# Pooled attention and a top-1 mixture of experts: one half of the values leaves undivided and is scaled after the gather

## The chip, the cores and the metric

The kernel runs on one core of a Trainium2 chip. The metric is the device time of one execution in microseconds (us), as the median of several runs. Five engines work side by side, each through its own instructions in order: TensorE (PE; PEld is its weight load), VectorE (DVE), ScalarE (ACT), GpSimd (POOL) and SyncE (SP, which here issues transfers). PE writes its sums to PSUM; DVE and ACT read them there, and POOL works on tiles in SBUF and issues the indirect transfers. L614 stands for line 614 of the kernel.

## The reference

Attention over keys and values that are averaged in groups of 8, then a mixture of experts in which each token goes to the one expert with the highest logit:

```python
# q, k, v: 8 batches x 8 heads x 576 x 64
k_p = k.reshape(B, H, 72, 8, D).mean(axis=3)
v_p = v.reshape(B, H, 72, 8, D).mean(axis=3)
scores = (q @ k_p.T) / sqrt(64); scores -= scores.max(-1)
attn = exp(scores); attn /= attn.sum(-1) + 1e-9
x = (attn @ v_p) -> 4608 tokens x 512 (the 8 heads side by side)

logits = x @ w_gate + modality_bias[modality_id]      # 8 experts
e_idx = argmax(logits); gate_w = softmax(logits)[e_idx]
for e in range(8):
    mask = e_idx == e
    h = max(x[mask] @ w1[e], 0)                       # 512 -> 1024
    out[mask] = gate_w[mask] * (h @ w2[e])            # 1024 -> 512
```

## The kernel before, in words

**Attention, about 0 to 192 us.** The 4608 tokens are 36 tiles of 128. Two batches make nine tiles and five steps (`steps`): four steps of two tiles, and in the middle one step of a single tile that holds the last 64 tokens of both batches. There are 20 steps. The order of the work is written out by hand in a loop `for n in range(N + 1)`, which in step `n` computes the scores of step `n` and the values of the tiles of step `n - 1` (`old[0]` and, if there are two, `old[1]`). Each engine runs its instructions in the order in which this loop issues them.

For one tile the stages are: `s_pe` (PE: scores, L520 or L526), `s_dve` (DVE: maximum L533, subtraction L536), `s_act` (ACT: exponentials L548 and L549), `t_pe` and `t_act` (PE transposes the exponentials, L555; ACT copies them from PSUM, L560), `t4_pe` and `t4_act` (the same for the fourth part of the keys, L567 and L574), and then `a_pe` and `x_dve`. `a_pe` multiplies with the values on PE: per bank of PSUM two multiplications L590 and one L594. There are two banks, `av0` for heads 0 to 3 and `av1` for heads 4 to 7, each a tile of its own with one buffer. For each head a bank holds 64 sums of values, 8 sums of logits (the values were multiplied by the gate's weights beforehand, in `v_gate`) and the sum of the exponentials.

`x_dve` divides on DVE, for each bank: L610 takes the sums of the exponentials times 8, L612 their reciprocals, L614 the 256 values times the reciprocals into a row `xb`, L616 the 32 logits times the reciprocals. Between them `gap` lets the next operations of the routing through (`drip`, DVE's list of routing work). SP stores the finished rows of `xb`, 528 columns wide, to a table `xs` in DRAM (L625); columns 512 to 527 hold the gate value and otherwise nothing that is used.

`v_gate`, once per batch, multiplies the pooled values with the gate's weights on PE into a spare part of a bank of scores, and writes them beside the values: two ACT instructions, and L387 on DVE for the fourth part. The next scores of that bank (L520 or L526) wait until these have read it. POOL folds the raw keys and values into their sums (L296 to L298).

**Experts, about 192 to 625 us.** The tokens are sorted by expert into slots of 256. The first two slots take tokens of the first 18 tiles (the groups 0 and 1, `EARLY_GROUPS` = 2) and are gathered while attention still runs. For every later slot POOL gathers the rows from `xs` by index, two indirect transfers of 128 rows (L142), at piece `f == 0` of the slot before (for slot 2 at `f == 3`). A slot has eight pieces `f`; each is the first layer (`hidden`, L162) and the second (`second`, L1143) on PE. At `f == 5` (`f == 6` for slot 2) PE transposes the next slot's rows (`x_transposes`, L153), and ACT and DVE split them into a high and a low part (L155, L156). ACT and DVE also split the weights of the next slot (L135, and L138 on DVE, 128 x 1024). POOL scatters the results (L1129).

Of the kernel before, what the change touches and what calls it, by code (L numbers as in the profile page):

```python
# [9 lines left out]
F32 = mybir.dt.float32  # L10
# [5 lines left out]
ALU = mybir.AluOpType  # L16
# [6 lines left out]
P = 128  # L23
SLOT = 256
EARLY_GROUPS = 2
# [5 lines left out]
def kernel(  # L31
# [37 lines left out]

    xs = dram.tile([NTOK, XW], F32, name="xs")  # L70

# [15 lines left out]
    xg = [cp.tile([P, XW], F32, name=f"xg{i}") for i in range(4)]  # L87
# [52 lines left out]
    def gather(s, idx, col, xgs, rows=NTOK):  # L140
        for tt in range(2):
            nc.gpsimd.indirect_dma_start(  # L142
                out=xgs[(2 * s + tt) % len(xgs)], out_offset=None, in_=xs[0:rows, :],
                in_offset=IndirectOffsetOnAxis(idx[:, col + tt:col + tt + 1].bitcast(U32), 0),
                bounds_check=rows - 1, oob_is_err=False)

    def x_transposes(s, xgs, tts=(0, 1)):
        a, b = xh[s % len(xh)], xl[s % len(xl)]
# [34 lines left out]
    with ExitStack() as actx:  # L183
        ap = actx.enter_context(tc.tile_pool(name="ap", bufs=1))

        late_p = actx.enter_context(tc.tile_pool(name="late_p", bufs=1))
        ps_av = actx.enter_context(tc.tile_pool(name="ps_av", bufs=1, space=PSUM))
# [166 lines left out]
        m4b = m_4.rearrange("p (j o) -> p j o", o=1)  # L354
# [19 lines left out]
        def v_gate(b):  # L374
            vt, vt4 = vts[b]
            dw, d4 = vw[b % NB], v4[b % NB]
            if b:
                pg = spare[1][:, 1, 4 * SPL:4 * SPL + 12 * E].rearrange("p (u x) -> p u x", u=3)
            else:
                pg = ps_tr.tile([P, 3, 4 * E], F32, tag="tr", name=f"pg_{b}")  # L380
            for u in range(2):
                nc.tensor.matmul(pg[:, u, :], vt[:, u, :], wgb[:, u].rearrange("p g x -> p (g x)"), start=True, stop=True)
            nc.tensor.matmul(pg[:, 2, :], vt4, wg[0:64, 1::2, :], start=True, stop=True)
            pgv = pg[:, 0:2, :].rearrange("p u (g a e) -> p (u g) a e", g=2, a=2)
            nc.scalar.activation(dw[:, :, 0, HD:HD + E], pgv[:, :, 0, :], AF.Copy, scale=m_a)
            nc.scalar.activation(dw[:, :, 1, HD:HD + E], pgv[:, :, 1, :], AF.Copy, scale=m_b)
            nc.vector.tensor_tensor(d4[:, :, HD:HD + E], pg[:, 2, :].rearrange("p (j e) -> p j e", j=NPAIR),  # L387
                                    m4b.to_broadcast([P, NPAIR, E]), op=ALU.mult)


        bias_all = ap.tile([P, NT, E], F32, name="bias_all")
# [89 lines left out]
        qts, pqs, scs, pes, pps, pts, avs, lgs = {}, {}, {}, {}, {}, {}, {}, {}  # L481
# [94 lines left out]
        def a_pe(t):  # L576
            n, z = tile_step[t]
            b, jj, _ = steps[n]
            pt, pt4 = pts.pop(t), pt4z[z]
            av = [ps_av.tile([P, 512], F32, tag=f"av{u}", name=f"av_{t}_{u}") for u in range(2)]  # L580
            avs[t] = av
            if jj is not None:
                halves = [(slice(0, P), b % NB)]
            else:
                halves = [(slice(64 * y, 64 * y + 64), (b - 1 + y) % NB) for y in range(2)]
            for u in range(2):
                for gg in range(2):
                    c = 2 * u + gg
                    for hs, y in halves:
                        nc.tensor.matmul(av[u][hs, 2 * VC * gg:2 * VC * (gg + 1)], pt[:, c, hs],  # L590
                                         vw[y][:, c].rearrange("p a x -> p (a x)"), start=(gg == 0), stop=False)
                dst4 = av[u][:, 0:4 * VC].rearrange("p (g x) -> p g x", g=2)[:, :, VC:2 * VC]
                for hs, y in halves:
                    nc.tensor.matmul(dst4[hs], pt4[:, hs], v4[y][:, 2 * u:2 * u + 2, :], start=False, stop=True)  # L594

        def x_dve(t):
            n, z = tile_step[t]
            g, gi = tile_group[t]
            av = avs.pop(t)
            mixed = steps[n][1] is None  # L600
            b = steps[n][0]
            if gi == 0:
                lgs[g] = late_p.tile([P, GT, H, E], F32, tag="lg", bufs=2, name=f"lg_{g}")
            xw = xbs[n if n < NX0 else NX0 + n % (len(xbs) - NX0)]
            xo = xw[:, z, 0:D]
            for u in range(2):
                avv = av[u][:, 0:4 * VC].rearrange("p (h x) -> p h x", h=4)
                r = ap.tile([P, 4], F32, tag="r", bufs=4, name=f"r_{t}_{u}")
                rb = r.rearrange("p (h o) -> p h o", o=1)
                nc.vector.tensor_scalar(r, avv[:, :, VC - 1], float(POOL), 1e-9 * POOL, op0=ALU.mult, op1=ALU.add)  # L610
                gap(1)
                nc.vector.reciprocal(r, r)  # L612
                gap(1)
                nc.vector.tensor_tensor(xo[:, u * D // 2:(u + 1) * D // 2].rearrange("p (h d) -> p h d", h=4), avv[:, :, 0:HD],  # L614
                                        rb.to_broadcast([P, 4, HD]), op=ALU.mult)
                nc.vector.tensor_tensor(lgs[g][:, gi, 4 * u:4 * u + 4, :], avv[:, :, HD:HD + E],  # L616
                                        rb.to_broadcast([P, 4, E]), op=ALU.mult)
# [277 lines left out]
        for n in range(N + 1):  # L895
            has, nxt, nxt2 = n < N, n + 1 < N, n + 2 < N
# [84 lines left out]
    op = [[ps_op.tile([P, 512], F32, name=f"op{i}_{z}") for z in range(2)] for i in range(2)]  # L981
# [75 lines left out]
    def row(a):  # L1057
# [201 lines left out]

    more(NSTAT - 1)  # L1260

# [29 lines left out]
```

## Time and profile before

| what | value |
|---|---|
| median of three runs | 641.79 us (639.85 to 642.85) |
| the profiled execution | 639.47 us, its span 637.8 us, granted clock 0.99 |
| PE busy | 601.1 us, 94% of the span |
| DVE busy | 433.8 us, 68% |
| ACT busy | 343.8 us, 54% |
| POOL busy | 198.9 us, 31% |
| the chain that ended last | PE 76%, DVE 13%, DMA 7% |

The busy share is an average over two phases with different limits, so a stage is read from a table by stretches of time. A row "PE av L590 <- DVE lg L616" in the table of waits says that PE, at line 590, which writes the tile `av`, was released by DVE's line 616. In the groups, "xb<-av,r 128x256" is an operation that writes `xb` from `av` and `r`, with 128 partitions of 256 elements; then come the count, the busy time in us, the mean in ns, and the idle time before. In the timeline the columns are the start, the length, the engine, the line and the operation, and in brackets the idle time before it and what ended it.

### The profile page before, as it was taken

Reading aid. Unit: us, or ns where it says so; the run is one execution under the profiler, and the core shown is the slowest. Engines: PE = TensorE matmul, PEld = TensorE weight load, DVE = VectorE, ACT = ScalarE, POOL = GpSimd, SP = SyncE. Lnnn points to the kernel's source line nnn. Section 1 sums busy time; section 2 is a strip of 40 time slices with the busy share of each in tenths; the row PEclk is TensorE's granted clock in tenths of the full one; section 3 lists DMA queues with packets and bytes.
Section 4 is the critical chain, followed back from the end, with each engine's and each line's share of the span. In section 5 each row is a group of like instructions: output and inputs, shape, how many; then the busy total and the mean of one; then the engine's idle time right before and its main releaser. Section 6 shows DMA issues by size and latency. Waiting matters only on the chain.

```text
span 637.8 us, 12547 instructions
## 1 busy us (share of the span) xinstructions
PE 601.1 (94%) x4223; PEld 544.8 (85%) x4223; DVE 433.8 (68%) x940; ACT 343.8 (54%) x640; POOL 198.9 (31%) x277
## 2 busy tenths in 40 slices
PE   4799898989899999999999999999999999999992
PEld 3699797888798999999999999999999999999881
DVE  4778989999977578666566566656656566656541
ACT  2667566677441455555555555555556555555530
POOL 6689967563000221320320221231131231131230
PEclk9899999999999999999999999999999999999997
DMA  9999979764201901201210461220225410120120
GB/s 255 290 300 337 350 208 362 223 202 143 67 35 51 315 33 36 68 34 35 68 41 28 148 201 51 67 65 8 63 75 180 145 55 17 52 68 18 51 75 17
DMA packets 63406, 77.18 MB, mean 121 GB/s; under 512 B 15455, under 2 KB 42079, under 8 KB 63328
## 3 DMA queue, kind: packets, MB, share of 16 engines
q1 hardware_dynamic: 57168, 55.98, 28.4%
q0 software_dynamic: 6160, 20.26, 9.7%
q8 instruction: 38, 0.62, 0.4%
q14 instruction: 40, 0.33, 0.2%
HBM read 119.94 MB, written 19.45 MB: 219 GB/s over the span
## 4 chain that ended last, share of the span: by engine, by line
PE 76%; DVE 13%; DMA 7%; issue 1%; ACT 1%; SPq 0%; DVEq 0%; ACTq 0%
PE op L1143 30%; PE hp L162 30%; DMA out_dram<-ob,sidx 6%; PE av L590 3%; PE sc L526 3%; PE xt L153 2%; DVE mx L533 2%; DVE sb L536 2%; PE av L594 2%; DVE xb L614 2%; PE pq L501 1%; PE ph L162 1%; PE pp L555 1%; DVE arow L717 1%; DMA k<-in_k_dram 1%
## 5 line engine op out<-in xcount | busy, mean ns | idle before, releaser
L135 ACT CAST hl<-raw 128x1024 fp32r<-128x1024 f32 x138 | 144.8, 1049 | 138.6 <-PE op L1143 136.6
L162 PE MATMUL hp<-xh,hl 128*128 128x256 f32 x1152 | 186.2, 284 | 0.6 <-issue 0.6
L162 PEld LDWEIGHTS hp<-xh,hl 128*128 128x128 f32 x1152 | 166.0, 189 | 11.5 <-issue 1.0
L138 DVE TENSOR_TENSOR hl<-raw,hl 128x1024 fp32r<-128x1024 f32 x144 | 174.8, 1215 | 0.0
L1143 PE MATMUL op<-hl,hh 128*128 128x512 f32 x554 | 173.5, 394 | 0.0
L1129 POOL DMA_INDIRECT out_dram<-ob,sidx x37 | 51.0, 1379 | 369.3 <-DVE ob L1125 260.2
L166 DVE SCALAR_TENSOR_TENSOR hlo<-hp,hh 128x256 fp32r<-128x256 f32 x139 | 58.8, 423 | 136.6 <-ACT hh L164 136.6
L1143 PE MATMUL op<-hl,hlo 128*128 128x512 f32 x277 | 108.4, 391 | 0.0
L1143 PEld LDWEIGHTS op<-hl,hh 128*128 128x128 f32 x554 | 94.8, 189 | 12.1
L162 PE MATMUL hp<-xl,hl 128*128 128x256 f32 x576 | 92.0, 282 | 0.0
L164 ACT ACTIVATE hh<-hp 128x256 fp32r<-128x256 f32 x139 | 53.4, 384 | 49.6 <-PE hp L162 49.6
L162 PEld LDWEIGHTS hp<-xl,hl 128*128 128x128 f32 x576 | 79.0, 190 | 0.0
L1143 PEld LDWEIGHTS op<-hl,hlo 128*128 128x128 f32 x277 | 52.0, 188 | 11.8
L590 PE MATMUL av<-vw,pt 128*128 128x146 f32 (+1 forms) x320 | 50.9, 299 | 4.9 <-DVE lg L616 3.7
L142 POOL DMA_INDIRECT xg<-xs,gidx x40 | 44.2, 1105 | 17.1 <-issue 8.9
L590 PEld LDWEIGHTS av<-vw,pt 128*128 128x128 f32 (+1 forms) x320 | 40.3, 183 | 7.9 <-DVE lg L616 4.9
L526 PE MATMUL sc<-kt,qt 128*128 128x144 f32 x256 | 38.3, 294 | 1.5 <-DVE rs L706 1.1
L526 PEld LDWEIGHTS sc<-kt,qt 128*128 128x128 f32 x256 | 34.1, 195 | 2.4 <-DVE rs L706 1.3
L156 DVE TENSOR_TENSOR xl<-xt,xh 128x512 fp32r<-128x512 f32 x38 | 24.5, 684 | 15.5 <-ACT xh L155 15.5
L560 ACT COPY pt<-pp 128x512 f32<-128x512 f32 x36 | 21.1, 586 | 25.4 <-PE pp L555 25.0
L533 DVE TENSOR_REDUCE mx<-sc 128x8 f32<-128x576 f32 (+1 forms) x40 | 27.7, 692 | 10.0 <-PE sc L526 7.6
L614 DVE TENSOR_TENSOR xb<-av,r 128x256 f32<-128x256 f32 x72 | 30.4, 422 | 1.6
(226 smaller groups left out, 710.5 us busy)
## 6 DMA issues: line engine op xcount, KB each, us to landing
raw<-in_moe_w_dram SPq DMA_DIRECT2D x304, 256.0 KB
xs<-xb SPq DMA_DIRECT2D x16, 528.0 KB
k<-in_k_dram SPq DMA_DIRECT2D x7, 1024.0 KB
v<-in_v_dram SPq DMA_DIRECT2D x7, 1024.0 KB
q<-in_q_dram SPq DMA_DIRECT2D x6, 1024.0 KB
q<-in_q_dram SPq DMA_DIRECT2D x4, 512.0 KB
v<-in_v_dram SPq DMA_DIRECT2D x16, 128.0 KB
xs<-xb SPq DMA_DIRECT2D x8, 132.0 KB
```

The lines of the kernel that those rows point to most:

```text
L135: nc.scalar.copy(hl[f][:, 0, :], raw[f])
L138: eng.tensor_sub(hl[f][:, 1, :], raw[f], hl[f][:, 0, :].bitcast(F32))
L142: nc.gpsimd.indirect_dma_start(out=xgs[(2 * s + tt) % len(xgs)], out_offset=None, in_=xs[0:rows, :], in_offset=IndirectOffsetOnAxis(idx[:, ...
L162: nc.tensor.matmul(ph, hl[f][:, w, d * P:(d + 1) * P], x[:, d, :], start=(n == 0 and d == 0), stop=(n == 2 and d == ND - 1))
L164: nc.scalar.activation(hh, ph, AF.Relu)
L166: nc.vector.scalar_tensor_tensor(hlo, ph, 0.0, hh.bitcast(F32), op0=ALU.max, op1=ALU.subtract)
L526: nc.tensor.matmul(dst, qt[:, i, :], kt[b % NB][:, :, h * SPL:(h + 1) * SPL], start=True, stop=True)
L533: nc.vector.reduce_max(mx, scv, axis=AX.X)
L590: nc.tensor.matmul(av[u][hs, 2 * VC * gg:2 * VC * (gg + 1)], pt[:, c, hs], vw[y][:, c].rearrange("p a x -> p (a x)"), start=(gg == 0), sto ...
L614: nc.vector.tensor_tensor(xo[:, u * D // 2:(u + 1) * D // 2].rearrange("p (h d) -> p h d", h=4), avv[:, :, 0:HD], rb.to_broadcast([P, 4, H ...
L1129: nc.gpsimd.indirect_dma_start(out=out[:, :], out_offset=IndirectOffsetOnAxis(idx.bitcast(U32), 0), in_=ob, in_offset=None, bounds_check=N ...
L1143: nc.tensor.matmul(o[tt], l[:, ts_], hl[f][:, w, D:2 * D], start=(f == 0 and n == 0), stop=(f == NF - 1 and n == 2))
```

## The change

In `x_dve` the two banks become one tile `av` of two banks with one buffer. One scaling, one reciprocal and one logits operation serve all eight heads. The values of heads 4 to 7 are divided by DVE as before. For tiles 0 to 17 so are those of heads 0 to 3; from tile 18 on, that is from the eleventh step, ACT copies these 256 columns into the row undivided, and the eight reciprocals are written to columns 520 to 527 of the row. After the gather, POOL multiplies the 256 columns in place by the row's first four reciprocals (`scale_half`, twice per slot from slot 2 on), at `f == 3` (`f == 5` for slot 2). Rows of early tiles hold the value 1 in those columns. In `v_gate`, DVE's L387 becomes an ACT copy to SBUF and a multiplication on POOL.

```diff
+    RX = D + 8
+    def scale_half(s, xgs):
+        for tt in range(2):
+            x = xgs[(2 * s + tt) % len(xgs)]
+            xv = x[:, 0:D // 2].rearrange("p (h d) -> p h d", h=H // 2)
+            nc.gpsimd.tensor_tensor(xv, xv, x[:, RX:RX + H // 2]...to_broadcast([P, H // 2, HD]), op=ALU.mult)
...
# v_gate
-            nc.vector.tensor_tensor(d4[:, :, HD:HD + E], pg[:, 2, :]..., m4b..., op=ALU.mult)
+            vg4 = ap.tile([P, NPAIR, E], F32, tag="vg4", bufs=1, name=f"vg4_{b}")
+            nc.scalar.copy(vg4, pg[:, 2, :]...)
+            nc.gpsimd.tensor_tensor(d4[:, :, HD:HD + E], vg4, m4b..., op=ALU.mult)
...
-            nc.gpsimd.memset(t[:, :, D:XW], 0.0)
+            nc.gpsimd.memset(t[:, :, D:XW], 1.0)
...
# a_pe
-            av = [ps_av.tile([P, 512], F32, tag=f"av{u}", name=f"av_{t}_{u}") for u in range(2)]
+            av = ps_av.tile([P, 2, 512], F32, tag="av", name=f"av_{t}")
...
# x_dve
-            for u in range(2):
-                avv = av[u][:, 0:4 * VC].rearrange("p (h x) -> p h x", h=4)
-                r = ap.tile([P, 4], F32, tag="r", bufs=4, name=f"r_{t}_{u}")
-                nc.vector.tensor_scalar(r, avv[:, :, VC - 1], float(POOL), 1e-9 * POOL, op0=ALU.mult, op1=ALU.add)
-                gap(1)
-                nc.vector.reciprocal(r, r)
-                gap(1)
-                nc.vector.tensor_tensor(xo[:, u * D // 2:(u + 1) * D // 2]..., avv[:, :, 0:HD], rb..., op=ALU.mult)
-                nc.vector.tensor_tensor(lgs[g][:, gi, 4 * u:4 * u + 4, :], avv[:, :, HD:HD + E], rb..., op=ALU.mult)
+            avv = av[:, :, 0:4 * VC].rearrange("p u (h x) -> p u h x", h=4)
+            s8 = ap.tile([P, 2, 4], F32, tag="r", bufs=4, name=f"r_{t}")
+            late = g >= EARLY_GROUPS
+            r = xw[:, z, RX:RX + H].rearrange("p (u h) -> p u h", u=2) if late else s8
+            nc.vector.tensor_scalar(s8, avv[:, :, :, VC - 1], float(POOL), 1e-9 * POOL, op0=ALU.mult, op1=ALU.add)
+            gap(1)
+            nc.vector.reciprocal(r, s8)
+            gap(1)
+            nc.vector.tensor_tensor(lgs[g][:, gi]..., avv[:, :, :, HD:HD + E], rb..., op=ALU.mult)
+            nc.vector.tensor_tensor(xo[:, D // 2:D]..., avv[:, 1, :, 0:HD], rb[:, 1]..., op=ALU.mult)
+            if late:
+                nc.scalar.copy(xo[:, 0:D // 2]..., avv[:, 0, :, 0:HD])
+            else:
+                nc.vector.tensor_tensor(xo[:, 0:D // 2]..., avv[:, 0, :, 0:HD], rb[:, 0]..., op=ALU.mult)
+            gap(2)
...
# run (a slot of the experts)
+                if f == (5 if s == 1 else 3) and nxt and not early:
+                    scale_half(s + 1, xg)
```

In the changed kernel the lines move: L610, L612, L616 and L614 become L622, L624, L626 and L628 (heads 4 to 7), L631 is ACT's copy of heads 0 to 3, L633 is DVE's division of them for early tiles, and L152 is POOL's scaling.

DVE's order at tile 25, the first of the fifteenth step, before. A row gives line, operation, what it writes and reads (with buffer numbers) and the shape; L782 to L784 are routing operations that `gap` let through:

```order
L610 TENSOR_SCALAR r_0_2194<-av_0_2167 128x4
L782 TENSOR_TENSOR sc_104<-oh,e0oh 128x144
L612 RECIPROCAL r_0_2194<-r_0_2194 128x4
L783 TENSOR_REDUCE s_1630<-sc_104 128x18
L614 TENSOR_TENSOR xb_177<-av_0_2167,r_0_2194 128x256
L616 TENSOR_TENSOR lg_1695<-av_0_2167,r_0_2194 128x32
L610 TENSOR_SCALAR r_1_2201<-av_1_2168 128x4
L784 SCALAR_TENSOR_TENSOR b_1632<-rh,s_1630 128x18
L612 RECIPROCAL r_1_2201<-r_1_2201 128x4
L784 SCALAR_TENSOR_TENSOR b_1632<-rh,s_1630 128x18
L614 TENSOR_TENSOR xb_177<-av_1_2168,r_1_2201 128x256
L616 TENSOR_TENSOR lg_1695<-av_1_2168,r_1_2201 128x32
```

And in the changed kernel, the same tile:

```order
L622 TENSOR_SCALAR r_2082<-av_2056 128x8
L800 TENSOR_TENSOR sc_104<-oh,e0oh 128x144
L624 RECIPROCAL xb_177<-r_2082 128x8
L801 TENSOR_REDUCE s_1550<-sc_104 128x18
L626 TENSOR_TENSOR lg_1614<-av_2056,xb_177 128x64
L628 TENSOR_TENSOR xb_177<-av_2056,xb_177 128x256
L802 SCALAR_TENSOR_TENSOR b_1552<-rh,s_1550 128x18 x4
```

Eight instructions of the tile have become four, one bank's division has left DVE, and the routing operations stand behind the tile rather than in it.

ACT's order behind the second tile of the same step, before; L338 and L339 copy keys, and L560 begins the next step:

```order
L338 COPY kt_134<-pk_1_2249 64x192
L339 COPY kt_134<-pk_1_2249 64x192
L560 COPY pt_2273<-pp_2268 128x512
L548 ACTIVATE pe_2275<-sb_0_2227 128x2x2x128
L549 ACTIVATE pe_2275<-sb_0_2227 128x2x32
L574 COPY pt_0_135<-sc_0_2213 64x128
L574 COPY pt_1_136<-sc_0_2213 64x128
```

And in the changed kernel, where L346 and L347 are the copies of keys, L569 is `t_act`, L557 and L558 are `s_act`, and L583 is `t4_act`:

```order
L631 COPY xb_177<-av_2115 128x256
L346 COPY kt_134<-pk_1_2128 64x192
L347 COPY kt_134<-pk_1_2128 64x192
L569 COPY pt_2152<-pp_2147 128x512
L557 ACTIVATE pe_2154<-sb_0_2111 128x2x2x128
L558 ACTIVATE pe_2154<-sb_0_2111 128x2x32
L583 COPY pt_0_135<-sc_0_2097 64x128
L583 COPY pt_1_136<-sc_0_2097 64x128
```

The copy of the tile's undivided half stands ahead of the next step's work. In the program it waits for L628 of the same tile, which writes the other half of the same row and is the last of DVE's instructions that read `av`; and the next `a_pe` waits for both.

POOL's order in the expert phase, before; `xg` are the gathered rows, and `ob` the results to be scattered:

```order
L1129 DMA out_dram<-ob_1_3402,sidx_95 4608x512
L142 DMA xg_82<-xs,gidx 128x528
L142 DMA xg_83<-xs,gidx 128x528
L1129 DMA out_dram<-ob_0_3638,sidx 4608x512
L1129 DMA out_dram<-ob_1_3643,sidx 4608x512
```

And in the changed kernel:

```order
L1147 DMA out_dram<-ob_1_3240,sidx_95 4608x512
L143 DMA xg_82<-xs,gidx 128x528
L143 DMA xg_83<-xs,gidx 128x528
L152 TENSOR_TENSOR xg_82<-xg_82 128x256
L152 TENSOR_TENSOR xg_83<-xg_83 128x256
L1147 DMA out_dram<-ob_0_3478,sidx 4608x512
L1147 DMA out_dram<-ob_1_3483,sidx 4608x512
```

The two scalings stand between a slot's gather and the scatter of the slot that is then computed. The orders of PE and SP are the same in both kernels.

More of the change, by code (lines that the diff above doesn't have):

```diff
@@ L145, in gather @@
                 bounds_check=rows - 1, oob_is_err=False)
+    def scale_half(s, xgs):
+        for tt in range(2):
+            x = xgs[(2 * s + tt) % len(xgs)]
+            xv = x[:, 0:D // 2].rearrange("p (h d) -> p h d", h=H // 2)
+            nc.gpsimd.tensor_tensor(xv, xv, x[:, RX:RX + H // 2].rearrange("p (h o) -> p h o", o=1).to_broadcast([P, H // 2, HD]),
+                                    op=ALU.mult)
     def x_transposes(s, xgs, tts=(0, 1)):
@@ L386, in v_gate @@
             nc.scalar.activation(dw[:, :, 1, HD:HD + E], pgv[:, :, 1, :], AF.Copy, scale=m_b)
-            nc.vector.tensor_tensor(d4[:, :, HD:HD + E], pg[:, 2, :].rearrange("p (j e) -> p j e", j=NPAIR),
-                                    m4b.to_broadcast([P, NPAIR, E]), op=ALU.mult)
+            vg4 = ap.tile([P, NPAIR, E], F32, tag="vg4", bufs=1, name=f"vg4_{b}")
+            nc.scalar.copy(vg4, pg[:, 2, :].rearrange("p (j e) -> p j e", j=NPAIR))
+            nc.gpsimd.tensor_tensor(d4[:, :, HD:HD + E], vg4, m4b.to_broadcast([P, NPAIR, E]), op=ALU.mult)
         bias_all = ap.tile([P, NT, E], F32, name="bias_all")
@@ L605, in x_dve @@
             xo = xw[:, z, 0:D]
-            for u in range(2):
-                avv = av[u][:, 0:4 * VC].rearrange("p (h x) -> p h x", h=4)
-                r = ap.tile([P, 4], F32, tag="r", bufs=4, name=f"r_{t}_{u}")
-                rb = r.rearrange("p (h o) -> p h o", o=1)
-                nc.vector.tensor_scalar(r, avv[:, :, VC - 1], float(POOL), 1e-9 * POOL, op0=ALU.mult, op1=ALU.add)
-                gap(1)
-                nc.vector.reciprocal(r, r)
-                gap(1)
[L614 to L617, printed above, removed]
+            avv = av[:, :, 0:4 * VC].rearrange("p u (h x) -> p u h x", h=4)
+            s8 = ap.tile([P, 2, 4], F32, tag="r", bufs=4, name=f"r_{t}")
+            late = g >= EARLY_GROUPS
+            r = xw[:, z, RX:RX + H].rearrange("p (u h) -> p u h", u=2) if late else s8
+            rb = r.rearrange("p u (h o) -> p u h o", o=1)
+            nc.vector.tensor_scalar(s8, avv[:, :, :, VC - 1], float(POOL), 1e-9 * POOL, op0=ALU.mult, op1=ALU.add)
+            gap(1)
+            nc.vector.reciprocal(r, s8)
+            gap(1)
+            nc.vector.tensor_tensor(lgs[g][:, gi].rearrange("p (u h) e -> p u h e", u=2), avv[:, :, :, HD:HD + E],
+                                    rb.to_broadcast([P, 2, 4, E]), op=ALU.mult)
+            nc.vector.tensor_tensor(xo[:, D // 2:D].rearrange("p (h d) -> p h d", h=4),
+                                    avv[:, 1, :, 0:HD], rb[:, 1].to_broadcast([P, 4, HD]), op=ALU.mult)
+            if late:
+                nc.scalar.copy(xo[:, 0:D // 2].rearrange("p (h d) -> p h d", h=4), avv[:, 0, :, 0:HD])
+            else:
+                nc.vector.tensor_tensor(xo[:, 0:D // 2].rearrange("p (h d) -> p h d", h=4),
+                                        avv[:, 0, :, 0:HD], rb[:, 0].to_broadcast([P, 4, HD]), op=ALU.mult)
+            gap(2)
             if mixed:
```

4 lines of the change are left out of this document (2 added, 2 removed).

## Prediction

> **What bounds the kernel now.** I began with the table by stages (stretch, length, busy time and instruction count of PE, PEld, DVE, ACT, POOL, granted clock, DMA share, GB/s), then asked each stage which wait of PE ends last, and only then for the durations of the operations that the change touches.
>
> ```profile
> span 637.8 us, 12547 instructions
> 60.00:118.00 58.00, 52.18 (x427) 46.25 (x425) 55.22 (x185) 35.86 (x98) 45.24 (x73) 1.00 0.92 299
> 118.00:160.00 42.00, 39.12 (x348) 35.98 (x347) 40.51 (x137) 32.31 (x82) 17.14 (x26) 1.00 0.60 191
> 160.00:180.00 20.00, 16.82 (x151) 15.48 (x150) 19.37 (x68) 9.06 (x22) 0.00 (x0) 1.00 0.16 43
> 200.00:580.00 380.00, 380.00 (x2520) 345.66 (x2519) 239.23 (x354) 205.81 (x304) 80.11 (x64) 1.00 0.24 79
> ```
>
> There are two regimes. From 60 to 180 us (attention) DVE is busy 115.1 of 120 us and PE leaves 5.8 + 2.9 + 3.2 = 11.9 us idle: this is all that a lighter DVE can win, since in the experts' phase, from 200 to 580 us, PE is full at a clock of 1.00. There every us by which PE is held up is added to the end, and DVE has 37% to spare. The waits of PE in 60 to 180 us (total, times, longest):
>
> ```profile
> PE av L590 <- DVE lg L616: 3.7, 4, 1.3
> PE sc L520 <- DVE vw L387: 3.5, 3, 1.3
> PE sc L526 <- DVE rs L706: 1.1, 1, 1.1
> PE pp L555 <- DVE xl L156: 0.7, 1, 0.7
> PE pp L555 <- DVE h L166: 0.6, 1, 0.6
> ```
>
> Two are touched: the sums av, whose banks DVE must read before PE may write the next tile, and the scores sc, whose bank holds the gate values of `v_gate` until L387 has run. Both name DVE. The last three (2.4 us) belong to routing and to the first expert slot; the change leaves them.
>
> **DVE's part of a tile.** The operations by form (busy, mean ns of one), with the rows nearest to what replaces them:
>
> ```profile
> L614 DVE TENSOR_TENSOR xb<-av,r 128x256 f32<-128x256 f32 x50 | 21.1, 421 | 0.9
> L616 DVE TENSOR_TENSOR lg<-av,r 128x32 f32<-128x32 f32 x50 | 8.9, 179 | 0.0
> L612 DVE RECIPROCAL r<-r 128x4 f32<-128x4 f32 x50 | 8.7, 174 | 0.8
> L610 DVE TENSOR_SCALAR r<-av 128x4 f32<-128x4 f32 x50 | 7.5, 149 | 0.0
> L370 ACT COPY vt<-pv 128x256 f32<-128x256 f32 x5 | 1.9, 373 | 0.1
> L361 POOL TENSOR_TENSOR vw<-vp,m 128x256 f32<-128x256 f32 x5 | 3.0, 607 | 7.0 <-PE pk L332 7.0
> ```
>
> A tile costs DVE 2 x (149 + 174 + 421 + 179) = 1846 ns. Afterwards there is one scaling and one reciprocal over 8 columns instead of 4 (149 and 174, a few ns more) and one logits operation over 64 columns: from 32 columns at 179 to 256 at 421 is 1.08 ns per column, so 214. With one or two 421 ns halves that makes 958 ns for tiles 18 to 35 and 1379 ns for the earlier ones. But instructions overlap, so I take the path from their starts:
>
> ```profile
> 138.54 0.15 DVE L610 TENSOR_SCALAR r<-av 128x4 f32<-128x4 f32 x1
> 138.60 0.59 ACT L560 COPY pt<-pp 128x512 f32<-128x512 f32 x1 [2.44 <-PE pp L555]
> 138.73 0.18 DVE L612 RECIPROCAL r<-r 128x4 f32<-128x4 f32 x1
> 138.94 0.42 DVE L614 TENSOR_TENSOR xb<-av,r 128x256 f32<-128x256 f32 x1
> ...
> 139.28 0.18 DVE L616 TENSOR_TENSOR lg<-av,r 128x32 f32<-128x32 f32 x1
> 139.38 0.15 DVE L610 TENSOR_SCALAR r<-av 128x4 f32<-128x4 f32 x1
> ...
> 140.19 0.55 ACT L574 COPY pt<-sc 64x128 f32<-64x128 f32 x2 [0.27 <-PE sc L567]
> 140.22 0.75 DVE L533 TENSOR_REDUCE mx<-sc 128x8 f32<-128x576 f32 x1
> ```
>
> The steps are 0.19, 0.21, 0.34 and 0.10 us per bank, 138.54 to 140.22 for both: 1.68. Afterwards, 0.19 + 0.21 + 0.13 (logits over 64) + 0.34 = 0.87 for a late tile (0.80 less) and 1.21 for an early one (0.47 less). In 60 to 180 us there are 10 early and 15 late tiles, so DVE is relieved of 4.7 + 12.0 = 16.7 us: more than PE's idle time. DVE stops being the bound, and what is late next decides.
>
> **What is late next.** Two things in the order of the changed program work against the gain. First, the two banks become one tile: PE's next L590 waits for the whole chain of DVE, where bank 0 used to come free after 0.84 us. For an early tile it now comes free 0.37 us later in the chain; the 0.47 us that each tile saves DVE goes about there, and I count it as nothing (bounds: all of it, the first rival, and a loss of 10 x 0.37 = 3.7). Second, from tile 18 on ACT's copy stands behind DVE's half of the same tile and, on ACT, ahead of the next step's L560, L548, L549 and L574 (transposed probabilities, exponentials, the copy of the fourth part). Before, these four ran beside DVE's part: L560 began 0.06 us after L610, and L574 ended at 140.74, 2.20 us after it. PE's L594 cannot begin without L574. Afterwards the path is in line: DVE's half ends 0.95 us after the start, the copy takes 0.37 (L370's row; DVE's 421 as the upper end), the four take 140.74 - 138.60 - 0.27 of waiting = 1.87, and two handovers of 0.1 (my reading of the starts) make 3.4 us: 1.2 longer.
>
> In a late step that DVE bounds, this part starts up to two tiles' savings earlier, 1.6, so 1.2 - 1.6 = -0.4 us; such a step is the one above, and I take 5 of the 9 steps with late tiles in the window so: -2.0. In the other 4 DVE is not what comes last, and only PE's own work covers the longer line:
>
> ```profile
> 123.25 0.26 ACT L574 COPY pt<-sc 64x128 f32<-64x128 f32 x1
> ...
> 124.02 0.42 PE L594 MATMUL av<-vw,pt 128*64 128x146 f32 x4
> ```
>
> Here L574 ends at 123.51, 0.5 us before L594 starts. So 1.2 - 0.5 = 0.7 at worst, nothing at best (an earlier DVE fills it); the middle, 0.4, x 4 = +1.6.
>
> **`v_gate`.** L387 becomes a small ACT copy and a multiplication on POOL. ACT comes just from L386, so the bank is released without waiting for DVE's queue. PE's 3.5 us on L387 cannot come back in full: behind it stand DVE's sums and subtractions, for which PE would wait next. I take somewhat over half, 2.0 (bounds 0 and 3.5). The POOL operation (below L361's 607 ns for 256 columns) delays the folding of keys and values behind it, which POOL, busy 17.1 of 42 us there, can afford.
>
> **The expert phase.** For each slot that is gathered late, POOL runs two multiplications in place, and the transposes (L153) now wait for POOL and not for the gather itself. The x152 below are 19 slots of 8; the first two hold early tokens, so 17 slots x 2 = 34 operations of 607 ns = 20.6 us on POOL, which has 300 us to spare. Free, wherever the rows have landed 0.61 + 0.25 (handovers and DVE's interference, assumed) before they are transposed. Times from issue to landing, the DMA row of a gather's second half each time ahead of its two lines of the timeline:
>
> ```profile
> L153 PE MATMUL xt<-ident,xg 128*128 128x128 f32 x152 | 20.1, 272 | 0.2 <-DMA xg<-xs,gidx 0.2
> xg<-xs,gidx POOLq DMA_INDIRECT x1, 3.4
> 568.13 1.01 POOL L142 DMA_INDIRECT xg<-xs,gidx  x1 [0.31 <-issue]
> 574.56 1.03 PE L153 MATMUL xt<-ident,xg 128*128 128x128 f32 x8
> xg<-xs,gidx POOLq DMA_INDIRECT x1, 5.2
> 358.85 1.01 POOL L142 DMA_INDIRECT xg<-xs,gidx  x1 [0.31 <-issue]
> 363.71 1.08 PE L153 MATMUL xt<-ident,xg 128*128 128x128 f32 x8
> xg<-xs,gidx POOLq DMA_INDIRECT x1, 4.3
> 594.40 1.01 POOL L142 DMA_INDIRECT xg<-xs,gidx  x1 [0.31 <-DMA out_dram<-ob,sidx]
> 598.80 0.63 PE L153 MATMUL xt<-ident,xg 128*128 128x128 f32 x4 [0.21 <-DMA xg<-xs,gidx]
> ```
>
> At 568 the rows land at 571.5, over 3 us before the second half (0.5 after the row's start) is transposed: free. At 359 and 594 they land 0.1 us before, so each pays 0.86 - 0.1 = 0.76; a third slot, gathered at 219, has 0.67 us by the same three rows (left out for room) and pays 0.2. All the others have over 1.2. Sum 1.7, and 0.7 for operations that meet a long one of DVE's in these three slots: +2.4 (bounds 1.7 and, by the last rival, 9.0).
>
> ```profile
> 109.33 1.80 DVE L669 TENSOR_TENSOR lgr<-lgr,m 128x72 f32<-128x72 f32 x1
> 109.79 1.25 POOL L296 TENSOR_TENSOR v<-v 128x512 f32<-128x512 f32 x1
> 154.63 0.23 DVE L669 TENSOR_TENSOR lgr<-lgr,m 128x72 f32<-128x72 f32 x1
> L138 DVE TENSOR_TENSOR hl<-raw,hl 128x1024 fp32r<-128x1024 f32 x144 | 174.8, 1215 | 0.0
> ```
>
> This is the interference: the same L669 takes 0.23 us alone and 1.80 beside a folding operation of POOL. L138, which reads two tiles as L669 does, takes 1.2 us and runs every 2.8 us. [...]
>
> **The sum.** Early tiles 0, `v_gate` -2.0, five steps -2.0, four steps +1.6, experts +2.4: 0.0. The profiled execution took 639.47 us, 1.7 more than its span and 2.3 less than the median of three; so 639.5 for such an execution and 641.8 us for the median. A difference under 0.5%, 3.2 us, can't be told from no change.
>
> **Rivals.**
> - *The saving reaches PE whole.* For it: DVE is named in both large waits, and 16.7 us go. Against it: the copy in line on ACT. PE's idle time less the 2.4 us that stay is 9.5; -9.5 + 2.4 = -7.1: 634.7 us.
> - *ACT's line decides* (slower). If x_dve starts only half of the 1.6 earlier, since PE and not DVE sets when the sums are ready, the late steps cost 5 x (1.2 - 0.8) + 4 x 1.2 = +6.8; with -2.0 and +2.4 it is +7.2: 649.0 us. It decides once the late steps lose over 2.8. For it: L560 waited 2.44 us for PE, so ACT runs close behind PE already. Against it: DVE is busy 40.5 of 42 us.
> - *The scales collide.* In the three tight slots both scales wait out an L138: 3 x 2 x 1.22 = 7.3 in place of 0.7, +6.6: 648.4 us. Against it: L138 covers 43% of the time, so all six meeting one is unlikely.
>
> **Chances.** As summed, 0.45 (own range 638.6 to 645.0); the whole saving 0.27; ACT's line 0.18; the collision 0.10. So faster 0.27, same 0.45, slower 0.28. The range leaves out about half of the first rival and half of the second: 635.0 to 648.5.
>
> **What the changed profile would show.** DVE's busy time in 60 to 180 us down by some 16; no wait of PE on the gate values; in its place PE waiting at L590 or L594 for ACT's copy, and ACT waiting for DVE's half at 18 copies; in the expert phase waits of the transposes on POOL of 1.5 to 3 us in all, in three slots. PE's idle time in 60 to 180 us would tell: 9 to 11 if I am right, 2 to 4 if the first rival is, over 15 if the second. I would be wrong too if the copy's place on ACT shifts which tile waits, since the count of steps of either kind is my judgment from one step of each.

## The result, and the profile after

The changed kernel takes 637.41 us (median of 20 runs, 634.45 to 640.43) against 640.27 us before (20 runs, 638.99 to 643.4): a ratio of 0.9948, interval 0.9935 to 0.996, or 3.3 us faster (the two medians differ by 2.9). The forecast was no change, 641.8 us; it started from a median of three runs that stands 1.5 us above that of the twenty. The profiled execution took 636.02 us.

The stretches of time (columns as in the prediction):

```profile
span 634.3 us, 12479 instructions
60.00:118.00 58.00, 53.26 (x448) 48.49 (x447) 49.21 (x147) 37.55 (x107) 45.30 (x75) 1.00 0.93 303
118.00:160.00 42.00, 39.76 (x339) 34.93 (x338) 34.64 (x104) 34.21 (x95) 18.59 (x29) 1.00 0.60 188
160.00:180.00 20.00, 19.52 (x176) 18.39 (x175) 16.57 (x49) 10.68 (x29) 0.00 (x0) 1.00 0.13 41
200.00:580.00 380.00, 379.29 (x2516) 344.94 (x2515) 238.46 (x347) 206.56 (x304) 107.70 (x96) 1.00 0.24 79
```

DVE's busy time from 60 to 180 us fell from 115.1 to 100.4 us, and PE's idle time from 11.9 to 7.5 us. That is less than the "9 to 11" at which the prediction would have been right, and more than the "2 to 4" of its first rival. The waits of PE in 60 to 180 us, and below them the expert phase's (from 180 us on):

```profile
PE av L599 <- DVE xb L633: 2.9, 2, 1.6
PE av L599 <- ACT pt L569: 1.9, 3, 1.0
PE xt L161 <- ACT qt L516: 1.0, 1, 1.0
PE sc L576 <- DVE sb L545: 0.7, 1, 0.7
PE av L599 <- ACT pt L583: 0.2, 1, 0.2
...
PE xt L161 <- POOL xg L152: 0.7, 1, 0.7
```

The wait on the gate values is gone. PE now waits for ACT at the sums (L569, L583), and once for POOL's scaling. Its largest wait is behind L633, the last of DVE's operations that read the joined tile in early tiles: this is the later release that the prediction named and counted as nothing. On the other side DVE and ACT wait more, in 105 to 190 us:

```profile
DVE r L622 <- PE av L603: 7.3, 9, 1.9
ACT xb L631 <- DVE xb L628: 10.4, 9, 2.2
```

DVE, which PE used to wait for, now waits for PE nine times in the late tiles; ACT stands 10.4 us at its copies until DVE's half is done. The late step at tile 24, the one of which the prediction showed the timeline, reads:

```profile
134.48 0.17 DVE L622 TENSOR_SCALAR r<-av 128x8 f32<-128x8 f32 x1 [1.21 <-PE av L603]
...
135.06 0.41 DVE L628 TENSOR_TENSOR xb<-av,xb 128x256 f32<-128x256 f32 x1
...
135.57 0.37 ACT L631 COPY xb<-av 128x256 f32<-128x256 f32 x1 [1.29 <-DVE xb L628]
...
135.84 0.59 ACT L569 COPY pt<-pp 128x512 f32<-128x512 f32 x1
...
136.48 0.77 PE L599 MATMUL av<-vw,pt 128*128 128x146 f32 x4
...
136.99 0.55 ACT L583 COPY pt<-sc 64x128 f32<-64x128 f32 x2
...
137.31 0.52 PE L603 MATMUL av<-vw,pt 128*128 128x146 f32 x2
```

This is the line that the prediction drew: DVE's half ends 0.99 us after L622 starts, the copy follows, then the four operations, and L583 ends 3.06 us after the start (3.4 forecast, 2.20 before). So the mechanisms were there; the sizes, and one reason, were not.

### The profile page after: what moved, and what is told of

Same layout as the page of the kernel before. It is cut to its first block, busy times and chain, and to the rows that moved or that the text cites. A ratio compares the mean times of both kernels' runs of the same rounds, so it can differ in the third digit from the quotient of the medians.

```text
span 634.3 us, 12479 instructions
## 1 busy us (share of the span) xinstructions
PE 601.2 (95%) x4223; PEld 544.1 (86%) x4223; DVE 412.4 (65%) x806; ACT 347.8 (55%) x666; POOL 231.2 (36%) x319
## 4 chain that ended last, share of the span: by engine, by line
PE 74%; DMA 12%; DVE 4%; ACT 3%; POOL 3%; issue 1%; SPq 1%; ACTq 0%; POOLq 0%; DVEq 0%
PE op L1161 29%; PE hp L170 29%; DMA out_dram<-ob,sidx 6%; DMA k<-in_k_dram 4%; PE av L599 4%; PE sc L535 2%; PE xt L161 2%; PE av L603 2%; PE pq L510 2%; PE ph L170 1%; PE pp L564 1%; DMA raw<-in_moe_w_dram 1%; DMA xg<-xs,gidx 1%; ACT pt L569 1%; DVE xb L628 1%
## 5 line engine op out<-in xcount | busy, mean ns | idle before, releaser
L139 DVE TENSOR_TENSOR hl<-raw,hl 128x1024 fp32r<-128x1024 f32 x144 | 175.2, 1218 | 0.0
L599 PE MATMUL av<-vw,pt 128*128 128x146 f32 (+1 forms) x320 | 49.9, 294 | 5.1 <-DVE xb L633 2.9
L152 POOL TENSOR_TENSOR xg<-xg 128x256 f32<-128x256 f32 x34 | 29.7, 876 | 36.4 <-DMA xg<-xs,gidx 36.3
L164 DVE TENSOR_TENSOR xl<-xt,xh 128x512 fp32r<-128x512 f32 x38 | 24.6, 685 | 16.8 <-ACT xh L163 16.8
L603 PE MATMUL av<-vw,pt 128*128 128x146 f32 (+1 forms) x160 | 30.8, 291 | 0.4
```

Of the source, the lines that this page charges most:

```text
L139: eng.tensor_sub(hl[f][:, 1, :], raw[f], hl[f][:, 0, :].bitcast(F32))
L152: nc.gpsimd.tensor_tensor(xv, xv, x[:, RX:RX + H // 2].rearrange("p (h o) -> p h o", o=1).to_broadcast([P, H // 2, HD]), op=ALU.mult)
L599: nc.tensor.matmul(av[hs, u, 2 * VC * gg:2 * VC * (gg + 1)], pt[:, c, hs], vw[y][:, c].rearrange("p a x -> p (a x)"), start=(gg == 0), sto ...
```

## The experiments

The times of kernels are told by their ratio to the kernel before, measured beside it; 0.1% is 0.64 us.

**The joining, the gate values, the scales, the release.** The first kernel is the change without the late split and with L387 on DVE; the second adds `v_gate`'s change; the third is the changed kernel without the scales; the fourth changes `before` alone.

```diff
# a1_pair and a2_pair_vgate (a1 also has v_gate as before)
-            late = g >= EARLY_GROUPS
+            late = False
...
# a3_noscale, and the two above
-                    scale_half(s + 1, xg)
...
# a4_onetile, from the kernel before
-            av = [ps_av.tile([P, 512], F32, tag=f"av{u}", name=f"av_{t}_{u}") for u in range(2)]
+            av2 = ps_av.tile([P, 2, 512], F32, tag="av", name=f"av_{t}")
+            av = [av2[:, u, :] for u in range(2)]
```

> The changed kernel with only the joining of the two banks: one scaling, one reciprocal and one logits operation per tile, both halves of the values divided by DVE in all 36 tiles; no copy on ACT, no scaling on POOL, and v_gate's last operation on DVE as before. By the forecast's step that an early tile's saving goes where its bank is released later, it stands within 1 us of the kernel before. By the rival that a lighter DVE reaches PE, 0.47 us in each of 36 tiles on a DVE that bounds the steps, it is 2 to 4 us faster than before.

Measured 0.9956 (0.9938 to 0.9974): 2.8 us faster. The rival holds: the joining isn't worth nothing.

> As the joining alone, and with v_gate's last operation as a copy on ACT and a multiplication on POOL. By the forecast (v_gate -2.0) it is 2 us faster than the joining alone. By the theory that PE's wait on the gate values only stands for a late DVE, it is within 0.7 us of the joining alone.

Measured 0.9892 (0.9872 to 0.9911), 633.12 us: 4.1 us beyond the joining alone, twice the forecast's term, and the best of all kernels here that compute the whole result. It is 3.6 us faster than the changed kernel: the late split costs more than it brings.

> The changed kernel without the multiplications on POOL after the gather; the values of heads 0 to 3 then stay undivided from tile 18 on. The forecast put the scales at +2.4 us: it would then be 2.4 us faster than the changed kernel. If the trace's single wait of 0.7 us on POOL is all that they cost, 0.5 to 1 us faster.

Measured 0.993 (0.9907 to 0.9952), 1.2 us below the changed kernel's 0.9948. By the times alone this is within their intervals; the traces add that PE's wait of 0.7 us at L161 is gone in this kernel and PE is busy 380.00 of 380 us.

> The kernel before with one thing changed: the two banks of sums are one tile, so that PE's next multiplications wait for DVE's last operation on the second bank, while DVE works bank by bank as before. By the forecast's bound for the later release (0.84 us later for the first bank, in the steps that DVE bounds) it is 2 to 4 us slower than before. If the release of the first bank was hardly used, it is within 1 us of before.

Measured 1.0079 (1.005 to 1.0107): 5.1 us slower, more than expected. Its row of waits in 60 to 180 us, against 3.7 us in four waits before:

```profile
PE av L591 <- DVE lg L617: 10.0, 10, 1.8
```

The later release is dear, then (up to 1.4 of the 5.1 us is a lower granted clock, as the last section works out), and the joining wins only because its shorter chain gives back 7.9 us.

**What in `v_gate` pays.**

```diff
# b1_vgate: v_gate's change alone, in the kernel before; d1_gate_dve_mult: the same but
-            nc.gpsimd.tensor_tensor(d4[:, :, HD:HD + E], vg4, m4b..., op=ALU.mult)
+            nc.vector.tensor_tensor(d4[:, :, HD:HD + E], vg4, m4b..., op=ALU.mult)
...
# e1_hold: the kernel before (L387 stays on DVE), with, behind L387,
...
+            nc.scalar.copy(vg4, pg[:, 2, :]...)
+            nc.gpsimd.tensor_tensor(vgs, vg4, m4b..., op=ALU.mult)
# e2_nohold: the same without the copy, from an operand that is long there
...
+            nc.gpsimd.tensor_tensor(vgs, vps[b][0][:, :, 0:E], m4b..., op=ALU.mult)
```

> The kernel before with v_gate's last operation alone moved to a copy on ACT and a multiplication on POOL. The forecast's term was -2.0 us. The joining with and without it differ by 4.1 us; if that is v_gate's own price, it is 4 us faster than before; if the joining was needed to free the time, because PE then only waits at the sums in place of the gate values, 1 to 2 us faster.

Measured 0.9905 (0.9885 to 0.9926): 6.1 us faster, by this edit alone, without any joining.

> The changed kernel with v_gate's last operation on DVE as before. If v_gate is worth 4 us whatever else is done, it stands at or above the kernel before (640 to 642 us). If the lighter DVE of the late tiles makes up for it, 638 to 639 us.

Measured 1.0027 (1.0008 to 1.0046): without `v_gate`'s edit, the rest of the change makes the kernel 1.7 us slower (a lower granted clock may be the whole of it, as the last section works out). Nothing is left of the change's gain.

> The kernel before with v_gate's last operation as a copy on ACT, which frees the bank, and the multiplication still on DVE, now from SBUF. With the multiplication on POOL this change was worth 5.7 us. If the earlier release of the bank of scores is what pays, it is 5 to 6 us faster than before; if DVE's freedom from standing behind ACT is what pays, 0 to 2 us.

Measured 1.0011 (0.9995 to 1.0027): nothing, and that refutes the release of the bank, the reason that the prediction gave. The bank is freed by ACT here, PE's wait on it shrinks, and it turns up again where the prediction said it would, behind DVE's sums and subtractions (PE's waits, 60 to 180 us; 3.7, 0.8 and 0.5 us before):

```profile
PE av L591 <- DVE lg L617: 3.7, 4, 1.3
PE av L591 <- DVE r L611: 1.9, 2, 1.0
PE sc L568 <- DVE sb L537: 1.2, 3, 0.6
```

So with the multiplication on POOL there must be something else. In the traces POOL then stands and waits for ACT at that operation (POOL's waits from 20 to 180 us, the changed kernel and then the experiment that has the pause alone):

```profile
POOL vw L397 <- ACT vg L396: 9.5, 3, 4.4
```

```profile
POOL vgs L392 <- ACT vg L391: 13.5, 5, 4.5
```

POOL stood still before, too, but elsewhere: between the foldings, for PE (the kernel before, then the pause alone):

```profile
POOL kp L298 <- PE pk L332: 16.7, 3, 7.4
```

```profile
POOL kp L298 <- PE pk L332: 3.6, 2, 1.8
```

So the new operation moves POOL's standing still rather than adding to it. The foldings of keys ahead of it run earlier and those of values behind it later (in one batch from 122.6 us in place of 126.0, and from 133.15 in place of 131.86), and some of DVE's routing operations run in the pause undisturbed. Two of them beside a folding, in the kernel before, and two in the pause:

```profile
131.05 2.29 DVE L717 TENSOR_SCALAR arow<-iota_b,rkf 128x128 bf16<-128x128 bf16 x2
...
131.86 1.26 POOL L296 TENSOR_TENSOR v<-v 128x512 f32<-128x512 f32 x1
```

```profile
129.30 0.24 DVE L721 TENSOR_SCALAR arow<-iota_b,rkf 128x128 bf16<-128x128 bf16 x1
...
129.54 0.22 DVE L721 TENSOR_SCALAR arow<-iota_b,rkf 128x128 bf16<-128x128 bf16 x1
...
132.95 0.24 POOL L392 TENSOR_TENSOR vgs<-vg,m 128x32 f32<-128x32 f32 x1 [4.53 <-ACT vg L391]
```

The groups of DVE from 60 to 150 us, for before, for the multiplication on DVE, for `v_gate`'s change alone and for the pause alone:

```profile
L717 DVE TENSOR_SCALAR arow<-iota_b,rkf 128x128 bf16<-128x128 bf16 x18 | 10.8, 622 | 0.0
L675 DVE TENSOR_TENSOR oh<-w,m 128x72 bf16<-128x72 f32 x2 | 2.6, 1312 | 0.0
```

```profile
L718 DVE TENSOR_SCALAR arow<-iota_b,rkf 128x128 bf16<-128x128 bf16 x18 | 10.2, 591 | 0.0
L676 DVE TENSOR_TENSOR oh<-w,m 128x72 bf16<-128x72 f32 x2 | 2.6, 1311 | 0.0
```

```profile
L718 DVE TENSOR_SCALAR arow<-iota_b,rkf 128x128 bf16<-128x128 bf16 x18 | 8.1, 470 | 0.0
L676 DVE TENSOR_TENSOR oh<-w,m 128x72 bf16<-128x72 f32 x2 | 0.5, 228 | 0.0
```

```profile
L721 DVE TENSOR_SCALAR arow<-iota_b,rkf 128x128 bf16<-128x128 bf16 x18 | 8.4, 487 | 0.0
L679 DVE TENSOR_TENSOR oh<-w,m 128x72 bf16<-128x72 f32 x2 | 0.5, 232 | 0.0
```

The same twenty instructions on the same engine take 13.4 us before, 12.8 with the multiplication on DVE, and 8.6 and 8.9 where POOL has paused. In 150 to 195 us, where POOL folds nothing, L717 takes 242 ns in the kernel before:

```profile
L717 DVE TENSOR_SCALAR arow<-iota_b,rkf 128x128 bf16<-128x128 bf16 x9 | 1.9, 242 | 0.0
```

> The kernel before, v_gate's L387 still on DVE, and beside it the copy on ACT and the multiplication on POOL as in the change, written to a tile that nobody reads. DVE is not relieved of anything and PE still waits for L387; all that is new is that POOL stands waiting for ACT and starts its next folding later. If that pause is what v_gate's 5.7 us come from (DVE's routing operations then run in it without a folding beside them: 10 to 11 us over their undisturbed times in the traces with the pause, 15 to 18 in those without), it is 3 to 5.5 us faster than before. If DVE's relief or the bank's release pays, it is within 1 us of before or slower.

Measured 0.9915 (0.9887 to 0.9943): 5.4 us faster, though DVE has lost no work and ACT and POOL have each got more. DVE isn't relieved here, the bank is released no earlier, and ACT's copy without POOL's wait brought nothing (the run with the multiplication on DVE). What is left as the cause is POOL's place in time.

> As the last, but the multiplication on POOL takes an operand that POOL has long made, so it doesn't wait: POOL has the same operation more and no pause, and there is no copy on ACT. If the pause pays, this one is within 1 us of before.

Measured 0.9956 (0.9941 to 0.9971): 2.8 us faster, where nothing was expected. A POOL operation that waits for nothing also shifts the foldings behind it, by its own length (238 ns in the mean), and that was enough for about half of the gain: the twenty routing operations take 10.3 us here. So what pays is which folding runs beside which routing operation, and not the pause as such. Summed over all DVE operations before 195 us, the time above the lower quartile of the same operation over the compared traces is about 17 us before, 17 with the multiplication on DVE, 14 here, 11 with `v_gate`'s change and 10 with the pause alone; the times relative to before go +0.7, -2.8, -6.1, -5.4. The two other pairs with and without `v_gate`'s edit agree: the sum falls by about 5 us on the joining (time -4.1) and by about 7 in the changed kernel (time -5.1).

**The late split.**

```diff
# b4_copytwice: the ACT copy a second time
+                nc.scalar.copy(xo[:, 0:D // 2]..., avv[:, 0, :, 0:HD])
# c1_copyfirst: the ACT copy moved ahead of DVE's scaling
# d2_drop: no ACT copy, no scales
# d3_z0 (d4_z1: z == 1)
-            late = g >= EARLY_GROUPS
+            late = g >= EARLY_GROUPS and z == 0
```

> The changed kernel with the copy on ACT and the scales on POOL both left out: from tile 18 on, the values of heads 0 to 3 aren't written at all (one buffer is filled at the start instead). It shows what the lighter DVE alone is worth in the late tiles. Against the joining with v_gate moved (633.1 us, both halves on DVE): if PE and not DVE bounds the late steps by then, within 1 us of 633; if the copy took back a real gain, 630 to 632 us.

Measured 0.9853 (0.9827 to 0.9878), 630.37 us: the lighter DVE alone is worth 2.5 us over the joining with `v_gate` moved. With the copy on ACT (the third kernel above, 0.993) 4.9 us are lost again. The stretch from 118 to 180 us shows it, for the joining with `v_gate` moved, the dropped half, the copy, and the copy twice:

```profile
118.00:180.00 62.00, 58.94 (x527) 54.93 (x526) 55.94 (x167) 43.22 (x111) 19.30 (x30) 1.00 0.48 152
```

```profile
118.00:180.00 62.00, 60.75 (x543) 56.81 (x542) 53.10 (x158) 43.78 (x112) 19.36 (x29) 1.00 0.45 148
```

```profile
118.00:180.00 62.00, 59.57 (x512) 53.41 (x511) 51.18 (x152) 45.25 (x123) 17.91 (x28) 1.00 0.43 135
```

```profile
118.00:180.00 62.00, 56.85 (x485) 50.21 (x484) 49.02 (x145) 48.02 (x130) 17.63 (x28) 1.00 0.43 139
```

With half a tile less on DVE PE finishes 543 multiplications in these 62 us, with the copy 512, with two copies 485. ACT is busy no more than 77% even in the last.

> The changed kernel with ACT's copy of heads 0 to 3 made twice in each tile from tile 18 on (18 times 0.37 us more on ACT). By the rival that ACT's line decides (copy after DVE's half, then the next step's four operations, then PE), some 13 steps' tiles lengthen the way to PE: 3 to 5 us slower than the changed kernel. By the forecast's reading that the line is covered in most steps, 0 to 1.5 us slower.

Measured 1.0017 (1.0 to 1.0033), 4.4 us above the changed kernel: the rival that ACT's line decides. 18 copies of 0.37 us are 6.7 us on ACT; about two thirds of it reaches the end.

> The changed kernel with ACT's copy issued ahead of DVE's four operations of the same tile; the copy then waits for PE's sums alone, and DVE's reciprocals (same row) wait for the copy. If the wait of the copy for DVE's half is what cost the late tiles their saving (2.4 us against the joining with v_gate moved), it is 2 to 3 us faster than the changed kernel, 634 to 635 us. If the ACT time itself costs it, or DVE now waits for an ACT that is busy, within 1 us of the changed kernel or slower.

Measured 1.0071 (1.0045 to 1.0096), 7.9 us above the changed kernel. Taking away the copy's wait for DVE wins nothing. Turned round, DVE waits for ACT, already at its scaling and not only at the reciprocals, and stops for longer (105 to 190 us):

```profile
DVE r L624 <- ACT xb L623: 17.8, 15, 2.5
...
620.62 0.66 ACT L172 ACTIVATE hx<-hp 128x256 fp32r<-128x256 f32 x2 [5.53 <-issue]
```

Only part of the 7.9 is that, though. The last gather starts 4.3 us later than in the changed kernel. Then, in the program's last stretch, ACT starts nothing for 5.53 us, waiting for nothing that the profile shows; PE waits 2.5 us for it, and its granted clock is 0.80 in the 6 us from 618 us and 0.91 in the next 6 (as much as 3.5 us at half would lose, an estimate). The profiled execution's span is 8.8 us longer, so some 4.5 us are lost there. In the kernel before and in the changed one ACT stops for 2.4 and 2.5 us at that place; why it is longer here stays open.

> The changed kernel with ACT's copy only for the first tile of a step (and the single tile of the mixed steps) from tile 18 on; second tiles are divided by DVE. Behind a first tile's copy stand the scores' exponentials of the same step, behind a second tile's copy the next step's transposed probabilities, for which PE waits soonest. If the copy hurts by standing ahead of those, this kernel is at the joining with v_gate moved plus the scales' 1.3 us: 634 to 635 us. If every copy costs alike, about 636.5 us.

> The changed kernel with ACT's copy only for the second tile of a step from tile 18 on; first tiles are divided by DVE. If the second tiles' copies carry the cost, it is as slow as the changed kernel, 637 us or more. If every copy costs alike, about 635.5 us.

Measured 0.993 (0.9907 to 0.9952) and 0.9937 (0.9914 to 0.9959), 1.2 and 0.7 us below the changed kernel, each with the scales. Both lie between the times forecast for copies that cost alike and for a dear second copy, and the intervals cover either: the runs don't decide it.

**A second pause.** In the joining with `v_gate` moved, a small copy on ACT and a small POOL operation that waits for it, once more per batch.

> The joining with v_gate moved (633.1 us), and a second pause per batch: in the steps where the next batch's values are folded, a small copy on ACT and a small multiplication on POOL that waits for it. If every pause of POOL lets DVE's routing through, 1 to 4 us faster, 629 to 632 us. If the pauses matter only where they happen to meet a routing operation, or the folding then comes late for PE, within 1 us of 633 or slower.

Measured 0.9891 (0.9871 to 0.9912), as without it (0.9892). In its trace POOL waits 15.7 us at the new operation, but only 2.0 at `v_gate`'s, against 8.5 without it: this second pause mostly takes the first one's place, and gives nothing more.

## Why the prediction was wrong, point by point

The kernels form a chain, and the measured steps along it are the joining -2.8, `v_gate` -4.1, the lighter DVE of the late tiles -2.5, ACT's copy +4.9, the scales +1.2. They add up to the -3.3 us of the change because each is the difference to the kernel before it; this confirms nothing, and in another order the parts are other (`v_gate` is -6.1 alone and -5.1 in the changed kernel). Each difference carries an uncertainty of about 2 us. The forecast's 0.0 came as near as it did because its errors had both signs, which is luck; the first rival's whole saving of 7.1 us did not arrive either. For the tiles as a whole it had 0 - 2.0 + 1.6 = -0.4, and the chain has -2.8 - 2.5 + 4.9 = -0.4, though no single part agrees; what is left of the miss is `v_gate`, 2.1 too little, and the scales, 1.2 too much.

- *The step whose reason failed* is `v_gate`, -2.0 forecast, -4.1 to -6.1 measured (on the joining, and alone). The prediction took PE's 3.5 us on L387 as the source of the gain and halved it for what would be late next. That caution was right for the release of the bank, which brings nothing (the run with the multiplication on DVE). The gain came from the sentence that the prediction passed over: that POOL "can afford" the delay of the foldings. It had quoted L669 at 0.23 us alone and 1.80 beside a folding, used the pair for the expert phase, and never asked what moving the foldings does to these rows. The run with the pause alone shows it: with DVE's work and the bank's release as before, twenty routing operations take 8.9 us in place of 13.4, and the kernel is 5.4 us faster.
- *Early tiles at nothing.* Both opposing terms were named, but they don't cancel: the joining is worth 2.8 us over all 36 tiles, some 1.4 of it for the 18 early ones (an estimate by their number). One tile for two banks, without the shorter chain, costs 5.1 us over all 36; the bound of 3.7 was for ten tiles and a release 0.37 us later, where this run's comes 0.84 us later, so the two can't be compared directly.
- *Late tiles, -2.0 and +1.6.* The line through ACT is as drawn, but the count of steps was a guess, and its sum of -0.4 held these tiles' share of the joining. Measured, DVE's relief brings 2.5 beyond the joining and the copy takes 4.9: +2.4 against the joining, or about +1.0 with half of the joining's gain counted in (an estimate). The mechanism of the second rival, ACT's line, is at work and the late split loses by it; its price of +6.8 was too high, and `v_gate` hid the loss in the total.
- *The experts, +2.4.* Measured about 1.2, which the intervals don't tell from nothing. The 17 pairs of scales are there, and one slot pays: the second scale for slot 2 took 1.67 us in place of the first one's 0.66 because it met L138 (L139 in the changed kernel), and PE waited 0.7. The timeline there, and the two groups from 200 to 600 us:

```profile
218.17 0.66 POOL L152 TENSOR_TENSOR xg<-xg 128x256 f32<-128x256 f32 x1 [2.27 <-DMA xg<-xs,gidx]
...
219.44 1.22 DVE L139 TENSOR_TENSOR hl<-raw,hl 128x1024 fp32r<-128x1024 f32 x1
219.46 1.67 POOL L152 TENSOR_TENSOR xg<-xg 128x256 f32<-128x256 f32 x1 [0.62 <-DMA xg<-xs,gidx]
221.18 0.66 PE L161 MATMUL xt<-ident,xg 128*128 128x128 f32 x4 [0.71 <-POOL xg L152]
```

```profile
L139 DVE TENSOR_TENSOR hl<-raw,hl 128x1024 fp32r<-128x1024 f32 x132 | 160.8, 1218 | 0.0
L152 POOL TENSOR_TENSOR xg<-xg 128x256 f32<-128x256 f32 x34 | 29.7, 876 | 36.4 <-DMA xg<-xs,gidx 36.3
```

  The scales take 876 ns in the mean (609 the shortest, 616 the median), so collisions are common, and POOL bore them: the mean of L139 stays at 1218 ns. How long a scale stands beside an L138, which the 0.7 for collisions and the last rival use, no row of the kernel before shows. In the changed kernel the two scales that began within 0.03 us of the start of an L139 took 1.67 and 1.66 us, and the six in the three slots that were counted as tight took 2.5 us in all beyond 0.61 each, where the rival had 7.3. The tight slots of the profiled execution before were mostly that execution's gathers; they weren't tight in this one (the second scales at 357.66 and 593.45 us end 2.1 and 1.0 us before their rows are transposed). A margin read from one trace is one draw.
- *What held:* DVE's busy time fell by 14.7 us (16 forecast), the gate values' wait is gone, and PE now waits 3.1 us on ACT (0.2 before), beside 3.6 on DVE.

Two kinds of DVE's routing operations take longer where the foldings run: `oh` (L675), which reads two tiles, takes 1312 ns in the mean of 60 to 150 us in the kernel before and 228 with `v_gate`'s change, and `arow` (L717), a `tensor_scalar` with one input, 622 and, in 150 to 195 us, 242. Why the foldings hold them up the rows don't show. The prediction weighed such pairs only for the expert phase.

## What to carry to other kernels

Before costing a moved operation, list which operations of two engines slow each other, with both durations from the trace, and ask of every edit how it shifts one against the other: here a small operation that makes POOL wait was worth as much (5.4 us) as all the work taken off DVE (2.8 and 2.5). An engine that is busy no more than 77% can still set the time, if its operations stand in line between two that are waited for: doubling the suspected operation told that at once (4.4 us for 6.7 us of copies). And do one part at a time: a change with several parts came out at -3.3 us, and leaving the late split out gave -6.9.

## What the runs showed of the hardware

In two of the slower kernels the clock granted to PE fell behind waits of PE. From 72 to 80 us, the kernel before and the kernel with one tile for both banks:

```profile
72.00:80.00 8.00, 6.46 (x55) 5.77 (x53) 7.59 (x29) 3.90 (x10) 7.36 (x11) 1.00 1.06 356
```

```profile
72.00:80.00 8.00, 6.20 (x40) 5.41 (x40) 7.02 (x24) 3.17 (x11) 7.45 (x11) 0.79 1.06 364
```

PE is busy about as long but gets 40 operations done instead of 55, at 0.79 of the clock. In the trace of the kernel before such a dip is 3.4 us at 0.50 of the clock (24.8 to 28.2 us), and 0.79 over 8 us is the same loss. It happened in three places of the attention phase of the kernel with one tile and in three of the changed kernel with L387 on DVE, so the 5.1 us of the one and the loss of the other are not only their waits. Over their executions the mean granted clock is 0.9883 and 0.9887, against 0.9904 and 0.9913 for the kernel before beside them; by the difference in clock times the span (an estimate) that is at most 1.4 us of the one's 5.1, and as much as the other's 1.7. It isn't reserved to slower kernels: ten of the 17 profiled executions have such a dip, that of the fastest kernel, with the dropped half, among them. The kernel with the copy for first tiles and the one with a second pause show such dips in their profiled executions, which took 637.8 and 637.16 us against medians of 635.6 and 633.67; the kernel before has one at 24 to 32 us (0.79 over these 8 us), where the changed kernel, with PE's work from 17 us on starting at the same times within 0.1 us, has none. That seems to be chance, and a part of the 1 to 3 us by which executions of one kernel differ; no run here separates it.

What starts a dip isn't shown. The longest waits of PE ahead of one are 1.8 us in the kernel before (16.8 to 24.8 us), 1.8 in the kernel with one tile (64 to 80 and 105 to 148 us), 2.0 in the changed kernel with L387 on DVE (56 to 124 us), and the 2.5 us in the kernel with the copy first.
